# Exp and Ln from one activation table set, the set loads written out by the planner, and the late weights moved behind the last LN1 transpose

## The chip, the cores and the metric

The kernel runs on one core of one Trainium2 chip. The metric is the device time of the launch in microseconds (us). Times of the kernel before: 224.96, 220.78 and 222.47 us, median 222.47 us. One more execution was recorded by the profiler; its own time and its span are in the table below.

## The reference

One pre-LayerNorm block on x of shape (1, 2048, 448), bfloat16: sliding, dilated attention, then a spatial mixer with an MLP. `_layernorm` has no gain or bias.

```python
def _A_ref(x, wqkv, wo):                      # H = 16 heads of 28, W = 8, dil = 2
    q, k, v = split of x @ wqkv
    idx = pos[:, None] - arange(8) * 2        # each token sees 8 keys: itself, 2, 4, ... 14 back
    logits = q . k[idx] * 28 ** -0.5, masked where idx < 0
    return softmax(logits) @ v[idx] @ wo
def _B_ref(x, w1, w2, w3, w4):                # F = 1792
    h = gelu(layernorm(x) @ w1)               # four column groups shifted by -1, +1, -2, +2 tokens
    x1 = x + shifted(h) @ w2
    return x1 + gelu(layernorm(x1) @ w3) @ w4
h = x + _A_ref(layernorm(x), wqkv, wo)
out = h + _B_ref(layernorm(h), w1, w2, w3, w4)
```

## The kernel before, in words

**Tiling.** The 2048 tokens lie as 8 row pairs m = 0 to 7 of 2 x 128 tokens (even and odd tokens apart, since the attention's dilation is 2). For each m, `phase_LN1` normalizes on VectorE (tile `ln`) with 1/sqrt by a power on GpSimd (`vtmp`, `rstd`), and turns the result into `HT` (features on partitions): on TensorE for m = 0 and 1, by a DMA transpose on SP's queue for m = 2 to 7. These DMA transposes, and all later ones, are collected in the list `trs` (line 638), so `trs[0]` is that of m = 2 and `trs[5]` that of m = 7, the last of LN1. `phase_QK` (four column groups for each of four token groups u) and `phase_V` (nine token tiles) multiply from `HT`; ScalarE or VectorE copies the result from PSUM (`ps`) into `QK` and `vt`.

**Attention** is `phase_att` (line 681): nine groups (four column groups for g = 0, four for g = 1, one for g = 2). In each, TensorE makes the logits from `QK` in two halves, ScalarE takes Exp of each half into `pt` (128 x 912), VectorE multiplies by the band mask `msk`, TensorE sums with `ones` (the softmax sums), ScalarE takes **Ln** of the sums into `lnz` and then **Exp** of minus that (so the reciprocal is exp(-ln z)), TensorE multiplies `pt` by `vt`, and VectorE multiplies by `lnz` into `QK`. Then `phase_WO`, `phase_LN2` (again with DMA transposes), `phase_W1` with **Gelu** on ScalarE, `phase_W2`, `phase_LN3`, `phase_W3` with Gelu (into `h` or `arena`), and `phase_W4`, whose rows are stored by SP.

**Order of the work.** Nothing is issued in the order of the code. `_Sched` records every operation with its reads, writes and an estimated duration. `schedule()` (line 218) then simulates the five engines and picks, for each engine, the ready operation that can start first; among those within 100 ns of each other the one with the smaller `prio`. The priorities come from a handwritten list of phase names, `rank` (line 902). For ScalarE the planner also keeps the table set in use: an operation that carries a `table` other than the current one is charged `TABLE` = 1300 ns, and only `SWITCH` = 650 ns of it while candidates are compared. In `act` (line 467) Exp carries "exp" and Gelu carries "gelu"; Ln, Copy and the rest carry none. So the planner of before charges nothing for Ln. The table loads themselves are not written in this kernel: the build puts an `ACT_TABLE_LOAD` ahead of each activation whose function is not in the set that was loaded last.

**TensorE's fill.** `setup` also queues 36 matmuls on an empty tile (`ps<-pt`, 128 x 512, phase "warm"), which the planner places wherever its simulated TensorE is free.

**Loads.** `load_x` and the Q, K and V weights are issued at the start. The other weights are marked `bulk` (the planner paces them by an estimated queue) and may not be planned before the operation in `after` begins: here `after=trs[0:1]`, the DMA transpose of m = 2. They all go through SP's queue, which also carries the DMA transposes: wo (4 DMAs), w1 (4) and w2 (1) in `loads_b`, w3 (8) in `loads_c`, w4 (2 of 784 KB) in `loads_d`. In the rank list of before `loads_d` stands ahead of `loads_b`, and `loads_c` is last.

**Emission.** `emit` in `_plan` (line 1308) walks an engine's planned order and writes, for each operation, its waits and then its instructions; line 1314 writes every instruction, so all rows of the profile carry L1314. `_general_path` is a fallback behind a flag and does not run here.

Of the kernel before, what the change touches and what calls it, by code (L numbers as in the profile page):

```python
# [86 lines left out]
class _Sched:  # L87
# [85 lines left out]
    TABLE = 1300.0  # L173
    MODE = 90.0
    SLACK = 100.0
    SWITCH = 650.0
    LEAD = 500.0
    WINDOW = 3413.0

# [38 lines left out]
    def schedule(self):  # L218
# [58 lines left out]
        while done < n:  # L277
            best = None
            for e in engs:
                cand = None  # L280
                for op in ready[e]:
                    st = max(arr[op.idx][e], free[e])
                    if op.bulk:
                        st = max(st, qfree - self.LEAD)
                    if cand is not None and st > cand[0] + self.SLACK:
                        continue
                    if op.opts and any(max(t2, free[e2]) + op.opts[e2][1] < st + op.opts[e][1] for e2, t2 in arr[op.idx].items()):
                        continue
                    if op.groups and e == "pe":
                        taken = ()  # L290
                        for g in op.groups:
                            if g not in gbank:
                                at = place(g.n, st, taken)
                                if at is None:
                                    break
                                st = max(st, at[1])
                                taken += tuple(range(at[0], at[0] + g.n))
                        else:
                            at = True
                        if at is None:  # L300
                            continue
                    if e == "act" and op.table is not None and op.table != table:
                        st += self.SWITCH
                    if cand is None or st < cand[0] - self.SLACK or (st < cand[0] + self.SLACK and op.prio < cand[1].prio):
                        cand = (st, op)
                if cand is not None and (best is None or cand[0] < best[0]):
                    best = cand + (e,)
            if best is None:
                raise RuntimeError("no op can go: %r" % [(e, [(o.tag, o.idx) for o in ready[e]]) for e in engs])
            st, op, e = best  # L310
            for e2 in (op.opts or (op.eng,)):
                ready[e2].remove(op)
            i = op.idx
            eng_of[i] = e
            dur = op.opts[e][1] if op.opts else op.dur
            if e == "act" and op.table is not None:
                if op.table != table:
                    st += self.TABLE - self.SWITCH
                table = op.table
            if e == "pe":  # L320
                if op.mode != mode:
                    dur += self.MODE
                mode = op.mode
                dur = self.gated(ham, st, dur)
            op.t0 = beg[i] = st
            for g in op.groups:
                if g not in gbank:
                    b = place(g.n, st)[0]
                    gbank[g] = b
                    gleft[g] = len(g.ops)  # L330
                    g.bank = b
                    g.wait = set()
                    g.opener = op
                    for x in range(b, b + g.n):
                        g.wait |= {o for o in held_by[x] if o.eng != "pe"}
                        holder[x] = g
                        held_by[x] = []
                gleft[g] -= 1
                for x in range(gbank[g], gbank[g] + g.n):
                    held_by[x].append(op)  # L340
                    if gleft[g] == 0:
                        holder[x] = None
            if op.is_dma:
                free[e] = st + dur
                qfree = max(st + op.lat[0], qfree) + op.lat[1]
                op.t1 = qfree + op.lat[2]
            else:
                free[e] = st + dur + self.OCC[e]
                op.t1 = st + dur + self.LAT[e]
            fin[i] = op.t1  # L350
            order[e].append(op)
            self.gorder.append(op)
            done += 1
            for ch in self.children[i]:
                npend[ch.idx] -= 1
                if npend[ch.idx] == 0:
                    push(ch)
# [55 lines left out]
def _fast_path(nc, es, flag, A_x, A_wqkv, A_wo, B_w1, B_w2, B_w3, B_w4, out):  # L413
# [51 lines left out]
    SM = 8.2  # L465

    def act(out_ap, in_ap, func, n, **kw):
        table = {ACT.Exp: "exp", ACT.Gelu_apprx_tanh: "gelu"}.get(func)
        return S.add("act", "activation", 170 + n / 1.2, table=table, out=out_ap, in_=in_ap, func=func, **kw)

    def dve(meth, dur, **kw):
# [11 lines left out]
    def dma(chan, out_ap, in_ap, nbytes, dur=450.0, rate=200.0, q="sp", after=(), bulk=False):  # L483
        return S.macro(q, [("dma_start", dict(out=out_ap, in_=in_ap))], dur, chan=chan, lat=(1000.0, nbytes / rate, 1150.0),
                       after=after, bulk=bulk)
# [93 lines left out]
    def loads_b():  # L579
        S.tag = "loads_b"  # L580
        dma("msk", msk[half[1], 1, :], msk[half[0], 1, :], 64 * 912, after=first)
        dve("tensor_copy", 280, out=msk[:, 0, :], in_=msk[:, 1, :])
        for a in range(2):
            dve("memset", 70, ap=msk[0:7, 0, 4 * NQ * a:4 * NQ * a + NQ], constant=0.0)
        
        wov = A_wo.rearrange("(c j d) n -> j d c n", c=4, j=4)
        for j in range(4):
            dma("wo%d" % j, wo_s[32 * j:32 * j + 28, :, :], wov[j], D * D * 2 // 4, 600, rate=150.0, after=trs[0:1], bulk=True)
        wload("w1", w1_s[:, 0:KB * D].rearrange("p (b n) -> p b n", b=KB), B_w1, ("sp", "sp"), after=trs[0:1], bulk=True)
        dma("w2", w2_s[:], B_w2.rearrange("(c k) n -> k c n", k=112), D * D * 2, 620, rate=300.0, after=trs[0:1], bulk=True)  # L590

    def loads_c():
        S.tag = "loads_c"
        wload("w3", w3_s, B_w3, ("sp", "sp"), after=trs[0:1], bulk=True, each=True)

    def loads_d():
        S.tag = "loads_d"
        for f in range(2):
            dma("w4_%d" % f, w4_s[:, 7 * f:7 * f + 7, :], B_w4[896 * f:896 * f + 896, :].rearrange("(f k) n -> k f n", k=128), D * F,
                740, rate=333.0, after=trs[0:1], bulk=True)  # L600

    stc = [0]

# [241 lines left out]
    def w2_ln3(*ms):  # L845
# [17 lines left out]
    phase_V(3)  # L863
    phase_LN1(4)
    phase_LN1(5)
    loads_c()
    phase_LN1(6)
    phase_LN1(7)
    loads_d()
    phase_att(0)  # L870
    phase_QK(2)
# [28 lines left out]
    phase_W3(3)  # L900
    phase_W4(3)
    rank = {b: k for k, b in enumerate((
# [6 lines left out]
    ).split())}  # L909
    for op in S.ops:  # L910
        op.prio = 10000 * rank[op.tag] + op.idx
# [386 lines left out]
    return S  # L1298


def _plan(nc, es, S, prefix):
    order = S.schedule()
    S.settle()
    sems = {e: es.enter_context(nc.semaphore(prefix + "sem_" + e)) for e in order}
    chan_sems = {c: es.enter_context(nc.semaphore(prefix + "d_" + c)) for c in S.chan_count}
    plan = _emit_plan(S, order, sems, chan_sems)

    def emit(e, eng):
        out_final = {}
        for op in order.get(e, []):  # L1310
            for (sem, val) in plan[op.idx]:
                eng.wait_ge(sem, val)
            for meth, kw in op.ins:
                inst = getattr(eng, meth)(**kw)  # L1314
            if op.is_dma:
                inst.then_inc(op.sem, 16)
                if op.chan.startswith("out"):
                    out_final[op.chan] = max(out_final.get(op.chan, 0), op.val)
            elif op.users > 0:
                inst.then_inc(op.sem, 1)  # L1320

        def finish():
            for c, v in out_final.items():
                eng.wait_ge(chan_sems[c], v)
        return finish
    return emit
# [61 lines left out]
```

## Time and profile before

| | |
|---|---|
| the three timed runs | 224.96, 220.78, 222.47 us |
| the profiled execution's own time | 220.66 us |
| its span, first to last instruction | 218.9 us |
| mean granted TensorE clock | 0.949 |
| busy: TensorE / VectorE / ScalarE / GpSimd | 193.6 / 112.0 / 117.2 / 48.8 us |
| moved by DMA | 18.13 MB, mean 83 GB/s |

The span and the execution's own time differ by 1.8 us, which lies before the first and behind the last instruction. In the rows, PE is TensorE, PEld its weight loads, ACT is ScalarE, DVE is VectorE, POOL is GpSimd, SP is the engine that issues most DMAs. A row of the timeline shows the start, the duration, the engine, the operation with the tiles that it writes and reads, how many were merged, and in brackets the idle time ahead of it and what ended it. "issue" in these brackets means that nothing in the profile held the engine. The chain of waits is followed back from the last instruction, at each step to what released it.

### The profile page before, as it was taken

What the parts mean: (1) busy time and instruction counts of PE and PEld (TensorE: products, weight loads), DVE (VectorE), ACT (ScalarE), POOL (GpSimd) and SP (SyncE); (2) the same over time, 40 slices, a digit from 0 to 9 for tenths busy, and PEclk for the clock granted to TensorE, in tenths of its full rate; (3) what the DMA queues carried; (4) which work ended last, traced back from release to release, by engine and by line L of the source; (5) the groups of instructions that cost most, each with busy time, mean ns of one, the idle gap of its engine ahead of it and who ended that gap; (6) DMA issues with size and microseconds to landing.
All of it is one profiled execution on the core that took longest, in us unless ns stands there. A gap on an engine that the chain in (4) does not pass through costs nothing.

```text
span 218.9 us, 7400 instructions
## 1 busy us (share of the span) xinstructions
PE 193.6 (88%) x3391; PEld 129.1 (59%) x3391; DVE 112.0 (51%) x261; ACT 117.2 (54%) x119; POOL 48.8 (22%) x90
## 2 busy tenths in 40 slices
PE   7699785667799999749898999999999999999990
PEld 2368553245458865637485585578887558855540
DVE  5799652341469818833598916995100941012221
ACT  2276599827927999799838551017675003720000
POOL 6333200000007200920036301589000270000000
PEclk9999999656999999967999999999999999999998
DMA  6987999980002400610007230226100051001111
GB/s 217 325 256 135 206 186 256 353 290 11 4 0 48 87 3 3 70 21 6 0 0 89 44 84 3 42 49 144 23 3 0 3 126 45 0 3 42 42 42 52
DMA packets 29532, 18.13 MB, mean 83 GB/s; under 512 B 21112, under 2 KB 28600, under 8 KB 29496
## 3 DMA queue, kind: packets, MB, share of 16 engines
q1 hardware_dynamic: 28872, 16.58, 32.6%
q10 hardware_dynamic: 624, 1.03, 1.5%
q8 instruction: 27, 0.44, 0.8%
q14 instruction: 9, 0.07, 0.1%
HBM read 10.67 MB, written 1.84 MB: 57 GB/s over the span
## 4 chain that ended last, share of the span: by engine, by line
PE 64%; ACT 20%; DVE 5%; DMA 3%; POOL 3%; issue 3%
PE ps L1314 64%; ACT L1314 8%; ACT lnz L1314 7%; ACT pt L1314 2%; POOL rstd L1314 2%; DVE st L1314 2%; DMA xin<-in_A_x_dram 2%; ACT QK L1314 1%; DMA HT<-ln 1%; ACT vt L1314 1%; DVE xin L1314 1%; DVE QK L1314 1%; DVE ln L1314 1%; POOL vtmp L1314 1%; ACT h L1314 0%
## 5 line engine op out<-in xcount | busy, mean ns | idle before, releaser
L1314 PE MATMUL ps<-HT,w_s 64*128 64x256 bf16 (+1 forms) x1064 | 57.9, 267 | 1.4 <-ACT pt L1314 1.3
L1314 PEld LDWEIGHTS ps<-HT,w_s 64*128 64x128 bf16 x1064 | 49.7, 95 | 9.3 <-ACT pt L1314 1.4
L1314 DVE TENSOR_TENSOR xb<-ps,xb 128x448 bf16<-128x448 f32 (+1 forms) x24 | 18.4, 773 | 53.8 <-PE ps L1314 53.8
L1314 POOL TENSOR_SCALAR vtmp<-mv 128x2 f32<-128x2 f32 x32 | 6.4, 201 | 126.0 <-DVE mv L1314 124.6
L1314 ACT ACTIVATE arena<-ps 128x1024 bf16<-128x1024 f32 x14 | 14.3, 1024 | 34.4 <-PE ps L1314 34.4
L1314 ACT ACTIVATE QK<-ps 128x1024 bf16<-128x1024 f32 (+2 forms) x25 | 23.7, 956 | 12.1 <-PE ps L1314 11.9
L1314 PE MATMUL ps<-HT,arena 64*128 64x256 bf16 x448 | 27.5, 278 | 1.3 <-ACT lnz L1314 1.3
L1314 PEld LDWEIGHTS ps<-HT,arena 64*128 64x128 bf16 x448 | 21.7, 97 | 6.2 <-ACT lnz L1314 1.5
L1314 ACT ACT_TABLE_LOAD x18 | 23.1, 1283 | 2.6 <-issue 2.3
L1314 POOL TENSOR_TENSOR rstd<-vtmp,mhalf 128x2 f32<-128x2 f32 x32 | 22.1, 692 | 2.7
L1314 PE MATMUL ps<-w_s,h 128*128 128x448 bf16 x112 | 21.9, 353 | 0.9 <-ACT lnz L1314 0.9
L1314 ACT ACTIVATE pt<-ps 128x912 bf16<-128x912 f32 x18 | 15.9, 928 | 11.7 <-PE ps L1314 11.7
L1314 PE MATMUL ps<-w_s,arena 128*128 128x448 bf16 x112 | 21.5, 352 | 0.0
L1314 DVE TENSOR_TENSOR QK<-ps,lnz 128x456 bf16<-128x456 f32 (+1 forms) x24 | 11.0, 509 | 18.8 <-ACT lnz L1314 11.7
L1314 DVE BATCH_NORM_STATS2 st<-xin 128x6 f32<-128x448 bf16 x32 | 18.2, 610 | 1.3 <-DMA xin<-in_A_x_dram 1.1
L1314 ACT ACTIVATE h<-ps 128x1024 bf16<-128x1024 f32 x14 | 14.1, 1024 | 8.5 <-PE ps L1314 8.5
L1314 PEld LDWEIGHTS ps<-w_s,h 128*128 128x128 bf16 x112 | 10.8, 98 | 11.4 <-ACT lnz L1314 1.3
L1314 POOL TENSOR_TENSOR xb<-xb,xin 128x448 bf16<-128x448 bf16 x16 | 16.9, 1087 | 0.9 <-DVE ln L1314 0.9
L1314 PEld LDWEIGHTS ps<-w_s,arena 128*128 128x128 bf16 x112 | 11.0, 98 | 10.2
L1314 DVE TENSOR_SCALAR ln<-xin,mv,rstd 128x448 bf16<-128x448 bf16 x32 | 14.7, 500 | 2.9 <-POOL rstd L1314 2.6
L1314 DVE TENSOR_TENSOR pt<-pt,msk 128x912 bf16<-128x912 bf16 x18 | 11.0, 630 | 8.9 <-ACT pt L1314 8.9
L1314 PE MATMUL ps<-wv_s,HT 64*64 64x448 bf16 x252 | 13.3, 352 | 2.3 <-DVE QK L1314 1.2
(54 smaller groups left out, 171.3 us busy)
## 6 DMA issues: line engine op xcount, KB each, us to landing
w_s<-in_B_w_dram SPq DMA_DIRECT2D x6, 448.0 KB, 8.9
out_dram<-xb SPq DMA_DIRECT2D x8, 224.0 KB, 1.9
xin<-in_A_x_dram SPq DMA_DIRECT2D x7, 224.0 KB, 7.9
w_s<-in_B_w_dram SPq DMA_DIRECT2D x2, 784.0 KB, 6.4
h<-in_A_wqkv_dram ACTq DMA_DIRECT2D x1, 672.0 KB, 7.7
h<-in_A_wqkv_dram SPq DMA_DIRECT2D x1, 672.0 KB, 6.7
wv_s<-in_A_wqkv_dram SPq DMA_DIRECT2D x2, 336.0 KB, 8.6
w_s<-in_B_w_dram SPq DMA_DIRECT2D x2, 336.0 KB, 7.5
```

The lines of the kernel that those rows point to most:

```text
L1314: inst = getattr(eng, meth)(**kw)
```

## The change

Three things. (1) Ln gets the table "exp" in the planner, and the emitted program names the sets itself: "exp" is the set `natural_log_exp_and_others`, which holds both Exp and Ln, and "gelu" is `gelu_apprx_tanh_and_others`; the load is written ahead of the waits of the first operation that needs the other set. In the planner a load now runs while the engine waits (`max(st, free + TABLE)`), and the penalty while candidates are compared is 300 ns instead of 650. (2) wo, w1 and w2 move out of `loads_b` into `loads_w`; all of wo, w1, w2, w3 and w4 now come `after=trs[5:6]`, and their phases are recorded behind `phase_LN1(7)`. (3) The rank list is another one, so the planned order of all engines is another one. In the new list `loads_d` stands ahead of `loads_w`, that ahead of `loads_c`, and `LN1_6` and `LN1_7` stand ahead of both of the latter.

```diff
-    SWITCH = 650.0
+    SWITCH = 300.0
...
                     if e == "act" and op.table is not None and op.table != table:
-                        st += self.SWITCH
+                        st = max(st, free[e] + self.TABLE) + self.SWITCH
...
                 if op.table != table:
-                    st += self.TABLE - self.SWITCH
+                    st -= self.SWITCH
...
-        table = {ACT.Exp: "exp", ACT.Gelu_apprx_tanh: "gelu"}.get(func)
+        table = {ACT.Exp: "exp", ACT.Ln: "exp", ACT.Gelu_apprx_tanh: "gelu"}.get(func)
...
-        
+
+    def loads_w():
+        S.tag = "loads_w"
         wov = A_wo.rearrange("(c j d) n -> j d c n", c=4, j=4)
...
-    (wo, w1, w2, w3, w4:) after=trs[0:1], bulk=True
+    (wo, w1, w2, w3, w4:) after=trs[5:6], bulk=True
...
     phase_LN1(5)
-    loads_c()
     phase_LN1(6)
     phase_LN1(7)
+    loads_w()
+    loads_c()
     loads_d()
...
-        "att_0_0 att_0_1 WO_1 LN1_0 QK_1_1 QK_1_0 QK_1_2 LN3_2 QK_1_3 V_3 W2_1 WO_0 V_2 LN2_0 LN1_1 att_0_3 "
+        "V_3 QK_1_1 att_1_2 QK_1_0 W1_3 W3_3 att_0_1 W3_2 QK_1_2 att_0_0 W2_0 W3_0 V_2 WO_7 QK_1_3 loads_d "
...
+_TABLE_SETS = {"exp": "natural_log_exp_and_others", "gelu": "gelu_apprx_tanh_and_others"}
...
         out_final = {}
+        table = None
         for op in order.get(e, []):
+            if op.table is not None and op.table != table:
+                table = op.table
+                eng.preload_act_table_set(_TABLE_SETS[table])
             for (sem, val) in plan[op.idx]:
```

More of the change, by code (lines that the diff above doesn't have):

```diff
@@ L584, in loads_b @@
             dve("memset", 70, ap=msk[0:7, 0, 4 * NQ * a:4 * NQ * a + NQ], constant=0.0)
+    def loads_w():
+        S.tag = "loads_w"
         wov = A_wo.rearrange("(c j d) n -> j d c n", c=4, j=4)
         for j in range(4):
-            dma("wo%d" % j, wo_s[32 * j:32 * j + 28, :, :], wov[j], D * D * 2 // 4, 600, rate=150.0, after=trs[0:1], bulk=True)
-        wload("w1", w1_s[:, 0:KB * D].rearrange("p (b n) -> p b n", b=KB), B_w1, ("sp", "sp"), after=trs[0:1], bulk=True)
-        dma("w2", w2_s[:], B_w2.rearrange("(c k) n -> k c n", k=112), D * D * 2, 620, rate=300.0, after=trs[0:1], bulk=True)
+            dma("wo%d" % j, wo_s[32 * j:32 * j + 28, :, :], wov[j], D * D * 2 // 4, 600, rate=150.0, after=trs[5:6], bulk=True)
+        wload("w1", w1_s[:, 0:KB * D].rearrange("p (b n) -> p b n", b=KB), B_w1, ("sp", "sp"), after=trs[5:6], bulk=True)
+        dma("w2", w2_s[:], B_w2.rearrange("(c k) n -> k c n", k=112), D * D * 2, 620, rate=300.0, after=trs[5:6], bulk=True)
     def loads_c():
         S.tag = "loads_c"
-        wload("w3", w3_s, B_w3, ("sp", "sp"), after=trs[0:1], bulk=True, each=True)
+        wload("w3", w3_s, B_w3, ("sp", "sp"), after=trs[5:6], bulk=True, each=True)
     def loads_d():
@@ L599, in loads_d @@
             dma("w4_%d" % f, w4_s[:, 7 * f:7 * f + 7, :], B_w4[896 * f:896 * f + 896, :].rearrange("(f k) n -> k f n", k=128), D * F,
-                740, rate=333.0, after=trs[0:1], bulk=True)
+                740, rate=333.0, after=trs[5:6], bulk=True)
     stc = [0]
```

10 rows, old and new, of the table rank are left out of this document.

## The prediction

> **What bounds the kernel now.** I read the page first (engines, chain), then busy time by stretch, then the chain and the timelines inside the stretches that have idle time.
>
> ```profile
> PE 193.6 (88%) x3391; PEld 129.1 (59%) x3391; DVE 112.0 (51%) x261; ACT 117.2 (54%) x119; POOL 48.8 (22%) x90
> ...
> PE 64%; ACT 20%; DVE 5%; DMA 3%; POOL 3%; issue 3%
> PE ps L1314 64%; ACT L1314 8%; ACT lnz L1314 7%; ACT pt L1314 2%; POOL rstd L1314 2%; DVE st L1314 2%; DMA xin<-in_A_x_dram 2%; ACT QK L1314 1%; DMA HT<-ln 1%; ACT vt L1314 1%; DVE xin L1314 1%; DVE QK L1314 1%; DVE ln L1314 1%; POOL vtmp L1314 1%; ACT h L1314 0%
> ...
> L1314 ACT ACT_TABLE_LOAD x18 | 23.1, 1283 | 2.6 <-issue 2.3
> ```
>
> TensorE sets the end, but a fifth of the chain is ScalarE, and 8% is "ACT L1314" without a tile: table loads. There are 18, 1283 ns each.
>
> ```profile
> 24.00:58.70 34.70, 23.99 (x741) 14.82 (x728) 11.66 (x19) 26.41 (x27) 0.69 (x1) 0.80 0.79 188
> 58.70:89.70 31.00, 30.40 (x648) 20.86 (x648) 22.09 (x48) 24.71 (x28) 7.58 (x17) 1.00 0.12 25
> 89.70:120.00 30.30, 24.95 (x701) 17.78 (x702) 19.76 (x43) 23.83 (x24) 9.89 (x16) 0.89 0.27 34
> 120.00:214.00 94.00, 93.64 (x1037) 62.52 (x1037) 37.98 (x88) 30.26 (x30) 20.78 (x32) 1.00 0.17 40
> ```
>
> Columns: stretch, length, busy PE, PEld, DVE, ACT, POOL, granted clock, DMA share, GB/s. From 58.7 to 89.7 and from 120 on TensorE is full (0.60 and 0.36 us idle), so a shorter ScalarE is worth nothing there. Idle time is in the first stretch (34.70 - 23.99 = 10.71 us) and the third (5.35 us). Part of the busy time is no work either: 13 fill matmuls (the first row below, all of them in the first stretch), and pieces at half clock, 28 matmuls in 3.17 us where the same 28 take 1.70.
>
> ```profile
> L1314 PE MATMUL ps<-pt 128*128 128x512 bf16 x13 | 4.7, 478 | 0.0
> ...
> 47.80 3.17 PE L1314 MATMUL ps<-HT,arena 64*128 64x256 bf16 x28
> ...
> 54.33 1.70 PE L1314 MATMUL ps<-HT,arena 64*128 64x256 bf16 x28 [1.33 <-ACT lnz L1314]
> ...
> 97.28 3.17 PE L1314 MATMUL ps<-HT,w_s 64*128 64x256 bf16 x28 [1.31 <-ACT pt L1314]
> ```
>
> Fill: 4.7 us. Half clock: 2 x (3.17 - 1.70) = 2.9 us. So the most that any order could win is 10.71 + 0.60 + 5.35 + 0.36 + 4.7 + 2.9 = 24.6 us.
>
> **The change, part by part. (1) Loads that go.** The chain shows where loads sit on the path:
>
> ```profile
> 30.99 1.28 ACT L1314
> ...
> 32.29 0.93 ACT lnz L1314
> ...
> 33.24 1.28 ACT L1314
> ```
>
> A load stands ahead of each Ln (or pair of them), and another ahead of the Exp behind it. The chain holds 13 loads: six in the first stretch (30.99, 33.24, 35.60, 37.85, 52.05, 55.12), two in the second (80.01, 83.07), five in the third (92.76, 95.00, 99.83, 102.08, 117.70). With one set for Exp and Ln only changes to and from Gelu remain. In the order of before, Gelu runs in three bursts, so these loads would remain, and one at 122.32 ahead of the last burst:
>
> ```profile
> 2.32 1.28 ACT L1314 ACT_TABLE_LOAD   x1 [2.32 <-issue]
> ...
> 75.39 1.28 ACT L1314 ACT_TABLE_LOAD   x1
> ...
> 80.01 1.28 ACT L1314 ACT_TABLE_LOAD   x1
> ...
> 104.44 1.28 ACT L1314 ACT_TABLE_LOAD   x1
> ...
> 117.70 1.28 ACT L1314 ACT_TABLE_LOAD   x1
> ```
>
> Six remain. Twelve go: 12 x 1.283 = 15.4 us of ScalarE time.
>
> First stretch: six go, 6 x 1.283 = 7.70 us. Can TensorE use them? Its idle time there is ended by ScalarE's chain or by "issue":
>
> ```profile
> 26.76 0.28 PE L1314 MATMUL ps<-QK 28*64 28x57 bf16 x11 [1.29 <-issue]
> ...
> 37.88 0.70 PE L1314 MATMUL ps<-QK 28*64 28x57 bf16 x64 [1.77 <-ACT lnz L1314]
> ...
> 41.05 0.74 PE L1314 MATMUL ps<-pt,vt 64*32 64x57 bf16 x64 [1.93 <-ACT vt L1314]
> ...
> 47.09 0.78 PE L1314 MATMUL ps<-QK 28*64 28x57 bf16 x54 [2.09 <-issue]
> ...
> 94.41 0.52 PE L1314 MATMUL ps<-pt,vt 64*32 64x57 bf16 x39 [1.32 <-issue]
> ```
>
> The two "issue" gaps, 3.38 us, break a block of 64 matmuls in its middle, where no semaphore is awaited; no ScalarE time removes them. That leaves 10.71 - 3.38 = 7.33 us idle and 4.7 us of fill that stands in idle places, 12.0 us: more than 7.70. I take 7.70. Third stretch: four go (5.13 us), the fifth, at 117.70, is Gelu to Exp and stays. TensorE's idle time without its "issue" gap is 5.35 - 1.32 = 4.03 us; I take 4.03. Second stretch: 83.07 goes, but TensorE is full there: 0, covered by the Q, K, V and W1 matmuls; without this cover it would be 1.28. Sum: 11.73 us.
>
> **(2) Loads ahead of the waits.** In the trace of before they already start as soon as ScalarE is free:
>
> ```profile
> 122.32 1.28 ACT L1314 ACT_TABLE_LOAD   x1
> 127.13 1.02 ACT L1314 ACTIVATE QK<-ps 112x1024 bf16<-112x1024 f32 x1 [3.53 <-PE ps L1314]
> ```
>
> The load ends at 123.60, 3.53 us before its Gelu is released, and over all 18 the idle time ahead of a load is 2.6 us, of which 2.3 us is the very first. So writing the load ahead of the waits is worth 0, bounds 0 and 2.6 - 2.3 = 0.3. The six loads that remain cost what they cost now.
>
> The Trainium skill weighs a load higher: its page "ScalarE: Activation LUTs", section "What ACT_TABLE_LOAD costs", gives a load of about 1283 ns and a drain of about 1380 ns, 2.66 us for each switch. By it, twelve switches would be an estimated 31.9 us of ScalarE time, and the sum would stand at what TensorE can use, 220.66 - 12.0 - 4.03 = 204.6. The trace agrees with 1283 and shows no drain: the Ln of 32.29 ends at 33.22 and the load starts at 33.24, so the sum stays with the row.
>
> **(3) Weights behind the last LN1 transpose.** SP's queue now:
>
> ```profile
> 18.61 0.58 SPq L1314 DMA_DIRECT2D w_s<-in_B_w_dram  x1
> 19.44 6.44 SPq L1314 DMA_TRANSPOSE HT<-ln  x3
> 25.92 0.59 SPq L1314 DMA_DIRECT2D w_s<-in_B_w_dram  x1
> 26.55 1.28 SPq L1314 DMA_TRANSPOSE HT<-ln  x1
> 27.88 2.28 SPq L1314 DMA_DIRECT2D wo_s<-in_A_wo_dram  x4
> 30.19 8.19 SPq L1314 DMA_DIRECT2D w_s<-in_B_w_dram  x13
> ...
> 24.79 0.92 DVE L1314 TENSOR_SCALAR ln<-xin,mv,rstd 128x448 bf16<-128x448 bf16 x2 [1.09 <-POOL rstd L1314]
> ...
> PEld ps L1314 <- DMA HT<-ln: 0.6, 2, 0.4
> ...
> w_s<-in_B_w_dram SPq DMA_DIRECT2D x6, 448.0 KB, 8.9
> ...
> w_s<-in_B_w_dram SPq DMA_DIRECT2D x2, 784.0 KB, 6.4
> ...
> L1314 PEld LDWEIGHTS ps<-wo_s,QK x64: 95/98/99, 60.2 to 137.3; 128*128 128x128 bf16 x64
> ```
>
> Of the 19 weight DMAs only the two of w4 (784 KB) are ahead of the last LN1 transpose now. Moving them frees SP for 0.58 + 0.59 us and the transposes from their traffic, but TensorE waits for transposed rows 0.6 us in the whole run: gain 0 to 0.6. In return w4 (6.4 us to landing each) may come ahead of wo. wo is issued from 27.88 and first used at 60.2, or 60.2 - 7.7 = 52.5 after the gain above; even 2 x 6.4 = 12.8 us later it has 11.8 us for itself from 40.7. Loss 0. I take 0 for this part; w1 to w4 are needed later still, behind the matmuls of that stretch.
>
> **(4) The new order.** The planner now sees what Ln costs, and a switch counts 300 instead of 650 ns, so it may switch oftener: each further pair is 2 x 1.283 = 2.6 us of ScalarE, which has 34.70 - 26.41 + 7.70 = 16.0 us free in the first stretch; two pairs, fully exposed, would be 5.1 us. The trace cannot show the new order. Its bounds are -5.1 and what is left of the 24.6 us without the three "issue" gaps (4.7): 24.6 - 4.7 - 11.7 = 8.2 us of gain. I take 0.
>
> **Sum.** 220.66 (the profiled execution) - 7.70 - 4.03 = 208.9 us. The median of the timed runs, 222.47, is 0.8% above that execution, so the changed kernel's median may be up to 208.9 x 1.008 = 210.6; I give the middle, 209.7 us.
>
> **The rivals.**
>
> *The new order closes most gaps too.* For it: Ln's loads were invisible to the old plan, so TensorE was ordered for a ScalarE 15.4 us faster than it was. Against: a wait for VectorE or the transposes stands behind each. With 5 to 8.2 of the 8.2 us: 201.5 to 204.7.
>
> *The refill of instructions takes the place of the loads.* The three "issue" gaps all fall into blocks of tiny matmuls, and the rows of the queues show
>
> ```profile
> q8 instruction: 27, 0.44, 0.8%
> ```
>
> 27 packets of 16 KB. In attention TensorE runs through 64 matmuls and 64 weight loads in 0.70 us, and the waits for ScalarE give the refill its time. Take these away and more gaps of 1.29 to 2.09 us may open; four to seven of them at 1.3 give 209.7 + 5.2 to 9.1 = 215 to 219. Against: only 3 of 27 refills show a gap now. The Trainium skill's page "Runtime: NRT & Kernel Launch" (section "Instruction fetch mechanics") also has blocks of 16 KiB and calls the crossing mostly hidden; by that this rival would be 0.
>
> *The change doesn't do what it says.* If the build still puts a load ahead of each Ln or Exp, there are 18 or more and only the order differs: 220.7 to 222.5. For it: the loads of before are placed by the build. Against: a set that holds both functions serves both.
>
> *Slower: the gate on the last LN1 transpose.* All weights now hang on it. It is released by `ln` on VectorE (the last at 24.79); if the new order lets VectorE do masks or other rows first, it issues late, and wo is late behind it. At worst wo lands 12.8 us (w4) and 8.9 us (the median of the 448 KB pieces) behind the gate, and is needed at 52.5. So for a last transpose later than 30.8 each us is lost, if nothing else fills TensorE; from 43.6 on the gain of 222.47 - 209.7 = 12.8 us is gone, and for a transpose at 50 the time is 209.7 + 19.2 = 229. Against: LN1_7 stands ahead of `loads_w` in the new list, and its `ln` ends at 25.71 now, 18 us before that point.
>
> **How the numbers follow.** A measurement of this kernel tells about 2% from no change: faster means below 218.0. Forecast 0.60 (its own range 204 to 214); most gaps closed 0.14; refill 0.12 (half below 218.0); no fewer loads 0.07; gate 0.07 (0.06 of it over 2% slower). Faster 0.60 + 0.14 + 0.06 = 0.80; within 2% 0.06 + 0.07 + 0.01 = 0.14; slower 0.06. The range runs from 201 (all that an order can win but the "issue" gaps: 220.66 - 19.9 = 200.8) to 218, which leaves out the last two rivals and the worse half of the refill, 0.20.
>
> **What would show it.** Right: 6 to 10 table loads, none between an Ln and an Exp; ScalarE busy about 102 us; "ACT L1314" below 4% of the chain; the first use of wo near 52; TensorE still full behind the attention, for some 94 us; transposes of LN1 landing without the two w4 DMAs between them. Wrong: more than 12 loads; "issue" gaps of TensorE well over 4.7 us; waits of TensorE for DMA into wo or w; a tail of W3 and W4 with holes.

## The result, and the profile after

The changed kernel takes 213.99 us (median of 4 runs, 213.31 to 215.53) against 222.22 us for the kernel before: a ratio of 0.966, 95% interval 0.958 to 0.974. Measured again later the ratio was 0.958 (0.952 to 0.963). The profiled execution took 214.20 us, its span is 212.5 us. Ratios compare only executions in the faster of two states in which this kernel's executions fall; medians are of all of them. The forecast was 209.7, so the direction and the range held, and the median is 4.3 us above it: 8.2 us came of the 12.8 (from 222.47) that were forecast.

From the page of after: the engines, the chain, and the group of table loads (from the groups by line).

```profile
PE 191.6 (90%) x3391; PEld 129.2 (61%) x3391; DVE 111.5 (52%) x259; ACT 100.4 (47%) x107; POOL 48.3 (23%) x90
...
PE 77%; issue 6%; DMA 6%; DVE 5%; POOL 2%; ACT 2%; ACTq 0%
...
L1320 ACT ACT_TABLE_LOAD x4 | 5.1, 1283 | 2.4 <-issue 2.3
```

ScalarE fell from 20% of the chain to 2%, and the table loads from 18 to 4. Besides TensorE, "issue" and DMA rose, each from 3% to 6%. The waits of TensorE, before first, then after (total us, times, longest), show the exchange:

```profile
PE ps L1314 <- ACT lnz L1314: 5.1, 4, 1.8
PE ps L1314 <- issue: 4.7, 3, 2.1
PE ps L1314 <- DVE QK L1314: 2.6, 3, 1.2
PE ps L1314 <- ACT vt L1314: 2.4, 2, 1.9
...
PE ps L1314 <- ACT pt L1314: 1.7, 2, 1.3
```

```profile
PE ps L1324 <- issue: 11.4, 8, 4.8
PE ps L1324 <- DVE pt L1324: 1.4, 1, 1.4
PE ps L1324 <- DVE ln L1324: 0.9, 2, 0.5
PE ps L1324 <- DMA HT<-ln: 0.6, 1, 0.6
PE ps L1324 <- ACT HT L1324: 0.5, 1, 0.5
PE ps L1324 <- DVE QK L1324: 0.2, 1, 0.2
```

TensorE waited 5.1 + 2.4 + 1.7 = 9.2 us for ScalarE and waits 0.5 now. But it stands idle 11.4 us with nothing to wait for, in eight gaps. The timeline of TensorE in after shows seven of them, a piece at half clock, and the first use of wo:

```profile
32.69 0.94 PE L1324 MATMUL ps<-wv_s,HT 64*64 64x448 bf16 x14 [0.69 <-issue]
...
38.89 0.58 PE L1324 MATMUL ps<-pt,vt 64*32 64x57 bf16 x52 [2.05 <-issue]
...
45.91 2.07 PE L1324 MATMUL ps<-wv_s,HT 64*64 64x448 bf16 x17 [4.79 <-issue]
...
48.78 2.93 PE L1324 MATMUL ps<-HT,arena 64*128 64x256 bf16 x28
...
52.86 0.59 PE L1324 MATMUL ps<-pt,vt 64*32 64x57 bf16 x54 [0.80 <-issue]
...
56.32 0.29 PE L1324 MATMUL ps<-pt,vt 64*32 64x57 bf16 x26 [0.76 <-issue]
...
60.48 4.70 PE L1324 MATMUL ps<-wo_s,QK 128*128 128x448 bf16 x24
...
90.15 0.24 PE L1324 MATMUL ps<-pt,vt 64*32 64x57 bf16 x11 [0.68 <-issue]
...
93.61 0.62 PE L1324 MATMUL ps<-QK 28*64 28x57 bf16 x47 [0.76 <-issue]
```

Count the matmuls from one gap to the next. The same profile by stretches that run from gap to gap (columns: stretch, length, TensorE busy with the number of matmuls, clock, DMA share, GB/s):

```profile
32.70:36.85 4.15, 4.14 (x128) 1.00 1.12 297
38.80:41.20 2.40, 2.22 (x128) 0.98 1.16 278
52.80:55.60 2.80, 2.69 (x128) 1.00 0.02 6
90.10:92.90 2.80, 2.70 (x128) 1.00 0.02 6
```

Always 128 (from 45.91 on the trace has 127, and in the two long stretches 510 and 381, that is 4 x 128 and 3 x 128 less two or three records). A matmul and its weight load are two instructions, so each of these gaps comes at a 256th instruction. The reading is that TensorE has used up 256 before the next 256 are there; the runs with matmuls alone, below, test it. The instruction queue has 27 packets in 0.44 MB, as before: 16 KB a packet, which is 64 bytes for each of 256. From gap end to gap end it takes 56.32 - 52.86 = 3.46 us and 93.61 - 90.15 = 3.46 us where DMA is quiet, but 38.89 - 32.69 = 6.20 and 45.91 - 38.89 = 7.02 us while the weights load. The page's row of transfers in 40 slices of 5.3 us has its peak there, in the ninth slice (42.5 to 47.8 us):

```profile
GB/s 221 321 271 88 110 202 278 283 412 112 6 5 0 93 46 3 3 6 88 3 91 58 32 4 129 86 3 3 0 26 117 119 3 3 3 0 43 43 43 54
```

Last, SP's queue in after:

```profile
15.40 8.64 SPq L1324 DMA_TRANSPOSE HT<-ln  x4
24.09 0.59 SPq L1324 DMA_DIRECT2D w_s<-in_B_w_dram  x1
24.73 4.91 SPq L1324 DMA_TRANSPOSE HT<-ln  x2
29.68 0.59 SPq L1324 DMA_DIRECT2D w_s<-in_B_w_dram  x1
```

One w4 DMA still stands ahead of two LN1 transposes. `trs[5]` is the last in the order of recording (m = 7), but the new rank list has `LN1_6` and `LN1_7` ahead of `LN1_5` and `LN1_4`, and so the gate opened when two transposes were still to be issued.

### The profile page after: what moved, and what is told of

It reads as the page before. It is cut to its first block, busy times and chain, and to the rows that moved or that the text cites. A ratio compares the mean times of both kernels' runs of the same rounds, so it can differ in the third digit from the quotient of the medians.

```text
span 212.5 us, 7395 instructions
## 1 busy us (share of the span) xinstructions
PE 191.6 (90%) x3391; PEld 129.2 (61%) x3391; DVE 111.5 (52%) x259; ACT 100.4 (47%) x107; POOL 48.3 (23%) x90
## 4 chain that ended last, share of the span: by engine, by line
PE 77%; issue 6%; DMA 6%; DVE 5%; POOL 2%; ACT 2%; ACTq 0%
PE ps L1324 77%; DMA h<-in_A_wqkv_dram 4%; DVE xin L1324 2%; DMA HT<-ln 2%; POOL rstd L1324 1%; DVE QK L1324 1%; ACT lnz L1324 1%; DVE ln L1324 1%; DVE xb L1324 0%; DVE st L1324 0%; ACTq L1324 0%; ACT arena L1324 0%; ACT HT L1324 0%; POOL vtmp L1324 0%; DVE pt L1324 0%
## 5 line engine op out<-in xcount | busy, mean ns | idle before, releaser
L1324 PE MATMUL ps<-HT,w_s 64*128 64x256 bf16 (+1 forms) x1064 | 56.3, 264 | 0.8 <-DMA HT<-ln 0.6
L1324 PEld LDWEIGHTS ps<-HT,w_s 64*128 64x128 bf16 x1064 | 49.9, 94 | 7.1 <-DMA HT<-ln 0.9
L1324 ACT ACTIVATE QK<-ps 128x1024 bf16<-128x1024 f32 (+2 forms) x24 | 22.7, 951 | 25.9 <-PE ps L1324 25.8
L1324 PE MATMUL ps<-wv_s,HT 64*64 64x448 bf16 x252 | 14.8, 367 | 5.5 <-issue 5.5
L1324 PEld LDWEIGHTS ps<-wv_s,HT 64*64 64x64 bf16 x252 | 7.1, 110 | 11.1 <-issue 7.1
```

## The experiments

**Theory A (loads):** the time follows the loads that leave the chain, as the sum had it. **Theory B (refill):** TensorE's instructions come in blocks of 256, and where it uses one up faster than the next arrives, it stands idle; transfers of weights slow the arrival. **Rival C:** the gain is the new order's, and the gaps are its own. In the experiments the order of every engine is that of before or of after, with only what the diff shows; DMAs are moved behind the planner.

**One set in the order of before.** ScalarE's program names the sets; the plan is that of before.

```diff
+            need = _SETS.get(op.ins[0][1].get("func")) if e == "act" else None
+            if need is not None and need != table:
+                table = need
+                eng.preload_act_table_set(need)
```

> The order of before on every engine, with Exp and Ln from one set: only the table loads differ (about 6 instead of 18). The prediction's sum: the six loads of the first stretch and four of the third come off the path, 222.2 - 11.7 = 210.5 us, first use of wo near 52.5 us, 'issue' gaps of TensorE still about 4.7 us. Rival theory (refill): the waits for ScalarE hid the refill of TensorE's instructions, which come in blocks of 256 (128 matmuls with their weight loads), so 'issue' gaps grow to 8 us or more and the time stays at 213 to 218.

Measured: 216.31 us against 223.33, ratio 0.971 (0.963 to 0.980); 6 loads. TensorE's "issue" gaps grew from 4.7 to 9.6 us, at three old places of the order and a new one (the first row is the sum of the gaps, their number and the longest):

```profile
PE ps L1323 <- issue: 9.6, 4, 3.3
...
27.80 0.37 PE L1323 MATMUL ps<-QK 28*64 28x57 bf16 x11 [2.10 <-issue]
...
43.11 0.55 PE L1323 MATMUL ps<-pt,vt 64*32 64x57 bf16 x49 [3.10 <-issue]
...
49.58 0.79 PE L1323 MATMUL ps<-QK 28*64 28x57 bf16 x54 [3.31 <-issue]
...
60.33 4.71 PE L1323 MATMUL ps<-wo_s,QK 128*128 128x448 bf16 x24
...
93.76 0.46 PE L1323 MATMUL ps<-pt,vt 64*32 64x57 bf16 x39 [1.06 <-issue]
```

The gaps before x11 and x54 were 1.29 and 2.09 us; the one before x49 is new, and that before x39 went from 1.32 to 1.06. Six loads are gone ahead of 60 us, and the first use of wo stays at 60.3 (60.2 in before): in the first stretch the gaps (8.5 instead of 3.4 us), and the half clock behind them, took back what the loads gave. The gain came later: from the first use of wo to the last matmul it takes 209.94 - 60.33 = 149.6 us, in before 213.47 - 60.18 = 153.3, so 3.7 us, near the 4.03 of the sum. This split is that of two single executions, 217.20 and 220.66 us, only 3.5 us apart where the medians are 7.0 apart. B is as forecast; and gaps can grow without the new order, which C did not expect.

**The loads of two sets in the order of after.** The build places the loads, 20 of them.

```diff
-                eng.preload_act_table_set(_TABLE_SETS[table])
```

> The order of after on every engine, but with the loads placed by the build, one for Exp and one for Ln (about 18 to 20 loads). If the loads are what the change wins, and every one of the 12 or more that come back stands on the path: 214.0 + 15 = 229 us. Refill theory: part of the loads hides behind the refill gaps that the order of after has anyway (11.4 us of 'issue' gaps), so 218 to 224, with fewer us of 'issue' gaps. If instead the new order made the gain, 214 to 216.

Measured: ratio 0.994 (0.989 to 0.999), about 221.4 us. The group of table loads, and TensorE's gaps (in the profiled execution, the longest of the ten with 224.02 us):

```profile
L1323 ACT ACT_TABLE_LOAD x20 | 25.7, 1283 | 2.7 <-issue 2.3
...
PE ps L1323 <- issue: 11.6, 9, 4.4
```

So new order and late weights are worth 0.6% without the one set; the one set alone (the run above) 2.9%; both 3.4 to 4.2%. The 16 loads that came back are 20.5 us of ScalarE time and cost some 7 us, about a third. That is the time that B expected, but not by B's way: the gaps are 11.6 us, not fewer than the 11.4 of after. The loads that came back show in other waits instead: those of TensorE for VectorE and ScalarE are 9.3 and 2.7 us here, 2.5 and 0.5 in after. Of C, the half on the gain falls. The half on the gaps holds for this order: with the new order and the late weights they stand whether the loads are there or not.

**w3 and w4 behind the first WO matmul,** in after and in before:

```diff
+    gate = [op for op in order["pe"] if op.tag == "WO_1"][0]
...
+    for op in late:
+        op.deps.add(gate)
```

> After with the ten DMAs of w3 and w4 (3.1 MB) moved behind the first WO matmul, about 60 us, all else in the same order. Refill theory with traffic: the gaps of 2.05 and 4.79 us stand where the weights load at 300 to 412 GB/s; without that traffic each is 0.7 to 0.9 like the five gaps in quiet stretches, and the half clock behind the long one (2.5 us) goes too: 206 to 209 us. Refill without a part of the traffic, or gaps from something else: 213 to 215 and the gap of about 4.8 stays.

> Before with the same ten DMAs moved behind the first WO matmul, loads as in before. Refill theory with traffic: the two gaps in the loaded stretch (1.29 and 2.09) shrink to about 0.7 at most, but the chain of ScalarE takes part of that: 219 to 221.5 us. If the place of the weights is worth nothing, as the prediction had it: 222.

Measured: after 213.22 us, ratio 0.959 (0.951 to 0.968), hardly another time than after's; before 223.60, ratio 1.003 (0.999 to 1.007), no change, where 219 to 221.5 were expected. In after neither 206 to 209 nor "the gap stays" came true: it moved. TensorE and the slices of after with late w3 and w4:

```profile
38.40 1.13 PE L1339 MATMUL ps<-wv_s,HT 64*64 64x448 bf16 x17 [0.98 <-issue]
...
49.94 4.70 PE L1339 MATMUL ps<-wo_s,QK 128*128 128x448 bf16 x24
...
71.73 0.25 PE L1339 MATMUL ps<-pt,vt 64*32 64x57 bf16 x8 [6.48 <-issue]
```

```profile
GB/s 213 329 281 89 113 144 233 7 6 5 295 418 235 108 3 3 3 6 89 3 92 84 6 43 115 63 3 3 0 41 117 107 3 3 3 0 44 44 44 55
```

The gap of 4.79 before the x17 block is 0.98 now, and wo is first used at 49.9 instead of 60.5. Then the moved weights (418 GB/s in the twelfth slice, 57.7 to 63.0 us) hold up the next refills, and a gap of 6.48 us opens before x8, where after has 0.91. In before with late weights, likewise, the two gaps of 1.29 and 2.09 us are gone but for one of 0.29, and a new one of 5.44 us ends at 74.05. In both runs the dense load of weights held up a refill where it was put.

**w3 and w4 paced:** each of the ten DMAs waits for a TensorE operation of its own, in after and in before with one set.

```diff
+    for op, tag in zip(late, _GATES):
+        gate = [o for o in order["pe"] if o.tag == tag][0]
...
+        op.deps.add(gate)
```

> After with the ten DMAs of w3 and w4 paced: each waits for a TensorE operation of its own, from about 40 to 72 us, so that they no longer queue behind one another; all else in the same order. Refill behind queued weights: a refill meets at most one weight DMA, so no 'issue' gap above about 1.5 us, their sum 5 to 7 instead of 11 us, 205 to 209 us. If it is the amount of traffic and not the queue, the gap of 5 to 6.5 us appears somewhere again: 212 to 214.

> The order of before with one set for Exp and Ln (216.3) and the ten DMAs of w3 and w4 paced in the same way. Refill behind queued weights: the gaps of 2.10, 3.10 and 3.31 us shrink to 1 or less, so about 5 us go: 209 to 212, near the 210.5 that the prediction's sum of loads gave for this order. If the gaps come from the missing waits alone: 215 to 217.

Measured: after, paced: **210.20 us**, ratio 0.943 (0.936 to 0.950), below after's interval. The longest gaps, one by one and in sum, and the slices:

```profile
39.14 1.13 PE L1347 MATMUL ps<-wv_s,HT 64*64 64x448 bf16 x17 [1.52 <-issue]
...
47.90 0.29 PE L1347 MATMUL ps<-pt,vt 64*32 64x57 bf16 x26 [2.13 <-issue]
...
86.17 0.28 PE L1347 MATMUL ps<-pt,vt 64*32 64x57 bf16 x11 [1.77 <-issue]
...
PE ps L1347 <- issue: 7.6, 9, 2.1
```

```profile
GB/s 210 328 287 88 107 149 141 3 151 58 142 112 183 100 120 148 164 3 92 23 69 91 0 47 112 63 3 3 0 43 118 105 3 3 3 0 44 44 44 55
```

The same bytes at 58 to 183 GB/s (ninth to seventeenth slice) leave no gap above 2.13 us. The expectation was a little too good: 7.6 us of gaps instead of 5 to 7, none above about 1.5, and 205 to 209 us. The gap of 1.52 us stands where hardly anything else is moved (3 GB/s, eighth slice), the other two beside pieces in flight.

Before with one set, paced, is less clear: 215.17 us, ratio 0.966 (0.956 to 0.976) against 0.971 (0.963 to 0.980) without pacing. Two of its four executions, 212.20 and 214.26 us at a granted clock of 0.98, lie below all four without pacing (215.75 to 217.20); the other two, 216.07 and 217.90 us at 0.951 and 0.961, do not. In the profile, that of 212.20 us, the gaps are 7.0 instead of 9.6 us, the longest 1.87, and wo is first used at 50.8 instead of 60.3. That is what theory B says, in one execution; in the median the gain is not told from no change.

**The refill by itself.** Two kernels that only multiply: five runs of tiny matmuls, weights loading during the second (3584-byte rows of w3) and the fourth (896-byte rows of w4).

```diff
-  eng.matmul(out=ps[0:64, k % 2, 0:57], lhsT=qk[0:28, 0:64], rhs=qk[0:28, 64:121], start=True, stop=True)
+  j, h, c = k % 4, k // 4 % 2, k // 8 % 8
+  eng.matmul(out=ps[64 * h:64 * h + 64, j, 57 * c:57 * c + 57], lhsT=qk[32 * j:32 * j + 28, 0:64],
+             rhs=qk[32 * j:32 * j + 28, 64:121], start=True, stop=True)
```

> Leaves out the whole computation (the output is zeros): TensorE runs five runs of 768 matmuls of 28x57 from one tile, with nothing else but, during the second, 5.5 MB of w3 rows (3584 bytes each) and, during the fourth, 3.2 MB of w4 rows (896 bytes each). Refill theory: in the quiet runs 128 matmuls take about 3.45 us (27 ns each, 1.4 us of work and 2 us of gap); in the loaded ones 6 to 10 us for each 128. If the gaps have nothing to do with 256 instructions: no regular gaps, about 11 ns for each matmul.

> Leaves out the whole computation (the output is zeros). As the run of one repeated matmul before it, where each took 53 ns and 128 of them 6.9 us, too slow to meet the refill except under load (gaps of about 1 us); here they go round four row groups and two column groups as the attention's do, about 11 to 13 ns each, five runs of 1024. Refill theory: quiet, one gap in every 128 matmuls, 3.45 us from gap to gap (about 1.5 of work, 2 of gap); while weights load, 7 to 10 us from gap to gap. If no refill bounds it: no regular gaps.

In the first kernel each matmul takes 53 ns, not the 27 that were expected, 128 of them 6.9 us, and quiet runs have no gap; two gaps of about 1 us stand in the part that w3 loads. In the second:

```profile
4.79 2.16 PE L35 MATMUL ps<-QK 28*64 28x57 bf16 x223 [4.79 <-DVE zero L29]
9.09 1.33 PE L35 MATMUL ps<-QK 28*64 28x57 bf16 x128 [2.15 <-issue]
13.09 1.33 PE L35 MATMUL ps<-QK 28*64 28x57 bf16 x128 [2.67 <-issue]
16.82 1.33 PE L35 MATMUL ps<-QK 28*64 28x57 bf16 x128 [2.40 <-issue]
20.27 1.33 PE L35 MATMUL ps<-QK 28*64 28x57 bf16 x128 [2.12 <-issue]
...
40.84 1.33 PE L35 MATMUL ps<-QK 28*64 28x57 bf16 x128 [3.45 <-issue]
50.05 1.44 PE L35 MATMUL ps<-QK 28*64 28x57 bf16 x128 [7.88 <-issue]
...
58.33 1.33 PE L35 MATMUL ps<-QK 28*64 28x57 bf16 x128 [3.19 <-issue]
66.72 1.33 PE L35 MATMUL ps<-QK 28*64 28x57 bf16 x128 [7.06 <-issue]
...
120.29 1.33 PE L35 MATMUL ps<-QK 28*64 28x57 bf16 x128 [4.04 <-issue]
```

Quiet, 128 matmuls take 1.33 us and come every 3.45 to 4.0 us. While w3 loaded, two of the blocks came 50.05 - 40.84 = 9.2 and 66.72 - 58.33 = 8.4 us behind the one before, the others 3.45 to 4.8; while w4 loaded, one came 4.04 + 1.33 = 5.4 us behind. So blocks of 128 matmuls, and their delay beside loads, are shown without anything of the kernel around them.

The page "Runtime: NRT & Kernel Launch" of the Trainium skill, section "Instruction fetch mechanics", has the same blocks of 256 instructions and calls crossing them mostly hidden. The first half agrees with the 128 matmuls between gaps; the second holds for the large matmuls here (of the 94.00 us from 120 us on in before, TensorE is busy for 93.64) and not for the small ones.

**The place of w4.** After with its two w4 DMAs where before has them, one ahead of the third LN1 transpose and one ahead of the last, measured twice; the second time beside after itself.

```diff
+    w4 = [op for op in order["sp"] if op.tag == "loads_d"]
+    tr = [op for op in order["sp"] if op.tag.startswith("LN1")]
+    for op, nxt in zip(w4, (tr[2], tr[5])):
+        for lst in (order["sp"], S.gorder):
+            lst.remove(op)
+            lst.insert(lst.index(nxt), op)
```

> After with the two w4 DMAs at the places that they had before: one ahead of the third of the six LN1 transposes, one ahead of the last. The prediction valued this part of the change at 0 (0 to 0.6 us): 214.0 to 214.6. If the place of these two DMAs matters for the refill, less traffic is left behind the transposes, and the time falls to 211 to 213.

> After with the two w4 DMAs at the places that they had before, once more, beside after on the same chip. Prediction: the place of w4 is worth 0, so equal to after within 0.5%. Refill behind queued weights: 0.8 MB to 1.6 MB less stands behind the transposes, 1 to 3 us faster than after.

> The changed kernel once more, beside the others of this chip: 214 us, ratio 0.966.

Measured: 212.35 us, ratio 0.949 (0.940 to 0.957); again 212.82, ratio 0.953 (0.948 to 0.959), beside after with 214.88 and 0.958 (0.952 to 0.963). The medians are 1.6 and 2.1 us below those of after, but side by side the intervals overlap: the late place of w4 shows no gain; whether it costs is not settled.

**w4 early and w3 paced:** the last edit, and the pacing for the eight DMAs of w3 alone, with one gate changed.

```diff
+        _early(S, order)
+        _pace(S, order)
```

> After with the two w4 DMAs at the places that they had before (among the LN1 transposes, where TensorE runs large matmuls) and the eight DMAs of w3 paced, each behind a TensorE operation that stands at the start of large matmuls. Refill behind queued weights: gaps left mostly while wo, w1 and w2 load; 207 to 210 us, below the 210.2 of the kernel that paces w3 and w4. If pacing has given all it can: 210 to 211.

Measured: ratio 0.943 (0.936 to 0.949), the same as with w3 and w4 paced; the median of all six executions is 212.37 us. So w4 early added nothing to the pacing that can be measured. A gap of 3.15 us is left, again before x8, so other gates may still win something; none were tried.

## Why the prediction was right in direction and short in size

*The loads, step 1.* Right as a mechanism: the loads leave the chain, and TensorE's waits for ScalarE go from 9.2 to 0.5 us. The new order kept four loads, not six: only one Gelu burst lies inside the attention. ScalarE's busy time fell by 117.2 - 100.4 = 16.8 us.

*The step that failed* is "The two 'issue' gaps ... no ScalarE time removes them", by which 4.7 us of gaps were held constant while the loads went. They are 11.4 us in after, 6.7 more. Two runs show what opens them. With only the loads taken away (one set in the order of before) they grow from 4.7 to 9.6 us: there the waits for ScalarE had given the refill its time. With the loads left in and only the order and the place of the weights changed (two sets in the order of after) they are 11.6 us: the parts of the change that steps 3 and 4 put at 0 open them as well, and in that order the loads make hardly any difference to them. Either is enough; how the 6.7 us divide is not shown.

The term of the sum that it hits is the first stretch: 7.70 us were to bring the first WO matmul to 52.5; it came at 60.5 in after and at 60.3 in the order of before, so nothing of the 7.70 was left there. The other term, 4.03, is borne out by the order of before, with 3.7 us. With the gaps of after the sum would have been 220.66 - 11.73 + 6.7 = 215.6, against 214.20 in the profiled execution; the other 1.4 us are not traced (TensorE's waits for VectorE fell from 5.9 to 2.5 us, its busy time by 2.0). The forecast's own range was 204 to 214: that 213.99 lies in it, and 214.88 of the second measurement just outside, is luck as much as method.

*The refill rival* had a mechanism that the order of before bears out, at a chance of 0.12 and 215 to 219 us; the time fell between it and the forecast. It did not see that the new order opens the gaps by itself. Its counter-argument, 3 gaps in 27 refills, counted refills in all stretches. Of the 13 block ends between 32 and 94 us of after, 8 show a gap: there 128 matmuls, many of them tiny, can be over in 2.2 to 2.7 us.

*Loads ahead of the waits, step 2:* 0, as said; the loads before already started when ScalarE came free, and the four of after have 2.4 us of idle time ahead of them, 2.3 of it the first's. *Weights, step 3:* no wait for wo or w, as said. But "Loss 0" looked only at who waits for the weights, and not at what else shares the DMA engines: paced, the same weights cost 3 to 5 us less (ratio 0.943 against 0.966 and 0.958). And the transposes are not all ahead of w4. *The new order, step 4:* taken as 0; with the late weights it measured 0.6% (0.1 to 1.1).

*The slower rival* did not come: the gate opened early enough, with the first w4 DMA issued at 24.09 us. *No fewer loads* is refuted by the count.

*The base:* 220.66 was the quickest end of a kernel whose runs here go up to 226; scaling the sum to the median by half was too little, which is 1 us of the miss at most.

## What to carry to other kernels

A gap of an engine that waits for nothing, in the middle of a block, is worth counting: if the instructions between two such gaps are always the same number, look for instructions that come too late, and do not count such gaps as fixed when you remove a wait in front of them. Bulk loads beside small matmuls should be paced by the progress of the consumer, not only be late. Spreading the small matmuls between large ones might help too; no run here tried it. A gate on "the last" of a list means the last in the order of execution only if that order is the list's.

## What the runs showed of the hardware that was not expected

- A block of 256 TensorE instructions arrives every 3.45 to 4.0 us when DMA is quiet, and took up to 9.2 us beside a dense load of 3584-byte rows. Whether the length of the rows or the amount matters is not shown. From a rest of 3.0 to 4.8 us, 223 matmuls ran before the first gap; with the 33 ahead of the rest that is 256, two blocks. Whether more would be ready after a longer rest is not shown.
- A refill gap of 4.79 us also cost clock: behind it 28 matmuls took 2.93 us instead of 1.70 (the granted clock from 45.9 to 52.1 us was 0.56), as behind the waits of before.
- No drain shows at a change of table set, as the prediction had read from before: in after, a Gelu starts at 77.99 and the load ahead of it ran from 76.70 for 1.28 us.
